# The low halves of the experts' weights, all made on VectorE instead of half of them on GpSimd

## The chip, the core and the metric

The kernel runs on one core of one Trainium2 chip. The metric is the device time of one execution in microseconds (us).

## What is computed

Sliding-window attention (8 heads, the second four dilated by 4) over 4 sequences of 576 tokens gives `x`, 2304 tokens of 512. Each token goes to the one of 8 experts with the largest logit; the result goes through one more pair of dense layers. Cut to what matters:

```python
for e in range(E):                       # 8 experts, w1[e] 512 x 1024, w2[e] 1024 x 512
    mask = e_idx == e
    h = np.maximum(x[mask] @ w1[e], 0.0)
    out[mask] = gate_w[mask, None] * eom[mask, e, None] * (h @ w2[e])
...
h = x @ w_in                             # second mixture: 512 x 2048, then 2048 x 512
return np.square(np.maximum(h, 0.0)) @ w_out
```

## The kernel before, in words

The program has three stages on the core: attention and routing (to about 140 us of the span), the experts (about 140 to 391 us), and the second mixture (from about 391 us). This document is about the second.

**Two halves of each operand.** TensorE gets every float32 operand as two float16 parts, `hi` (the operand, scaled and rounded) and `lo` (what rounding left over), and makes three products: hi by hi, hi by lo, lo by hi. So the weights of each expert are loaded as float32 and split on the chip while TensorE works on the experts before. That is the background work.

**The experts' order.** The experts are taken by rising number of tokens: rank 0 to rank 7, with 248, 264, 284, 304, 320, 340, 380 and 440 token columns. For each rank (L1115 to L1149) there are two layers:

- layer 1 has 8 steps `f`: 12 matmuls on TensorE (L1121), then `hs` hi on ScalarE (L1124, ReLU) and `hs` lo on VectorE (L1125), then some background work (L1127), and in ranks 1 to 4 one step of the sorted tables (`sorted_tables`, called at L1129: small VectorE operations at L777, L781, L202 to L206, L955 to L998, two on ScalarE, and the 18 products of L993);
- layer 2 has 4 steps `c`: first one block of the next rank's tokens is transposed on TensorE (L938) and split (L940 on ScalarE, L941 on VectorE), then 24 matmuls (L1142), which run through all eight `f` of `hs`, three for each, in rising order, then the output's hi on ScalarE (L1147) and lo on VectorE (L1148), then background work (L1149). 

The gathers of the next rank's tokens (L930) are issued from GpSimd's queue at the start of layer 1.

**The background work.** A *unit* is one layer of one rank (u0, u1 for rank 0, u2, u3 for rank 1, and so on), cut into four *pieces* of 128 x 1024 float32, here written u3.1 for piece 1 of unit 3. A piece is loaded by a DMA of SyncE's queue (L307) into one of four stage buffers, which are used in turn, so that the load of a piece waits until the piece four before it has been split. `split_ops` (L278) knows several ways:

- "H" (units 0 and 1): two halves, each hi on ScalarE (L294) and lo on VectorE (L295);
- "D": the whole piece at once, `hi = scale * t` on ScalarE (L294), `lo = scale * t - hi` on VectorE (L295, one scalar_tensor_tensor);
- "Q": ScalarE scales the stage buffer in place (L282), ScalarE copies it to hi (L287), GpSimd subtracts, `lo = t - hi` (L288). Those are two entries in the list of background work, where D is one.

`unit` (L1047) chooses at L1052. The weights of the second mixture's first layer (S pieces, `piece64`, four entries each: L324, L328, L332 on VectorE, L337 on ScalarE with L338 on VectorE) are put between them.

**What sets the order.** Each engine runs its instructions in program order. `Stream.to` (L261) puts the background entries into the program: after step `f` or `c` of a layer, that fraction of the entries of the layer's list is issued. So on VectorE the order in a step `f` is: `hs` lo, the background's, the table step. On ScalarE: `hs` hi, the background's.

```python
def on_pool(n):                                   # L284
    nc.scalar.activation(out=half(hi, n), in_=sv, func=AF.Copy)                                   # L287
    nc.gpsimd.tensor_tensor(out=half(lo, n), in0=sv, in1=half(hi, n), op=ALU.subtract)            # L288
def on_dve(n):                                    # L291
    nc.scalar.activation(out=half(hi, n), in_=sv, func=AF.Copy, scale=scale)                      # L294
    nc.vector.scalar_tensor_tensor(out=half(lo, n), in0=sv, scalar=scale, in1=half(hi, n), ...)   # L295
ops = {..., "D": [on_dve(None)], "H": [on_dve(0), on_dve(1)], "Q": [scaled, on_pool(None)]}       # L298
```

Of the kernel before, what the change touches and what calls it, by code (L numbers as in the profile page):

```python
# [12 lines left out]
I32 = mybir.dt.int32  # L13
# [11 lines left out]
HH = H // 2            # heads per mask type  # L25
WIN = 32               # keys per query
DIL = 4
SEG = S // DIL         # dilated heads: tokens ordered by residue, SEG per residue
QB = 64                # queries per score block
KW = QB + WIN          # keys per score block  # L30
NM = S // QB
NT = B * S
NB = NT // P           # token blocks
# [5 lines left out]
# A round of the mixture takes experts by rising number of tokens, this many tokens at most of each;  # L39
# rounds follow until every expert's tokens are done. Where the first caps do, one round does.  # L40
CAPS = ((248, 264, 284, 304, 320, 340, 380, 440), (256, 272, 296, 320, 344, 368, 416, 512))
CAP = CAPS[1]
CM = -(-max(CAP) // P)                                    # blocks of an expert's tokens in a round
NC = E * CM
NR = max(-(-(NT // (E - r)) // CAP[r]) for r in range(E)) # rounds at most
XW = NT + max(CAP)

# Float32 operands go through the tensor engine as two float16 parts, hi + lo,
# of the operand times a power of two that centres it in float16's range.
X_S = 64.0             # x  # L50
WG_S = 64.0            # logits carry X_S * WG_S
W1_S = 32.0            # h then carries X_S * W1_S
W2_S = 64.0
Y_S = X_S * W1_S * W2_S
Y2_D = 1.0 / 64.0      # y into the second MoE
# [8 lines left out]
# The attention's steps as the engines get them, which overlaps blocks of queries, sequences, and the routing of  # L64
# the blocks that are done: step.number, +products that only keep the tensor engine busy, :engine.
# Loads: LQ of a head pair's q or k, LV of a block's values, GT of the gates' weights.
# A head pair's q or k: QI puts its heads side by side, T transposes a half, TC copies it out.
# A block of queries: S scores (SA, SB: by kind of head), MX maxima, EX exponentials, PT, PC their transpose.
# A block of tokens: PV output, XN division by the sums, ST store, XT transpose, XE, XL its two parts (0, 1: by kind).
# Routing: LG, LE logits, CE early blocks' experts, CC their counts, RC their places, F one-hot places, L0-L2 late logits.  # L70
# [40 lines left out]
def fused_kernel(ctx: ExitStack, tc: tile.TileContext, q, k, v, w_gate, w_ogate, w1, w2, w_in, w_out, out):  # L111
# [16 lines left out]
    # routing: logits by token, and what it is worked out with  # L128
    def bc(ap, n):
        """a column for each of n more elements"""  # L130
        return ap.unsqueeze(len(ap.shape)).to_broadcast(list(ap.shape) + [n])

    def rows(ap, n):
        """[P, m] for each of n blocks"""
        return ap.unsqueeze(1).to_broadcast([P, n, ap.shape[1]])

    L = const.tile([P, NB, 2 * E], F32, name="L")
    d = const.tile([P, NB, E], F32, name="d")             # logit - largest
    cand = const.tile([P, NB, E], F32, name="cand")
    mxl = const.tile([P, NB], F32, name="mxl")  # L140
    oh = const.tile([P, NB, E], F16, name="oh")           # 1 at the token's expert
    iota = const.tile([P, 32], F32, name="iota")
    iota_h = const.tile([P, P], F16, name="iota_h")
    iota_n = const.tile([P, E], F32, name="iota_n")       # e - E
    tokc = const.tile([P, NB], F32, name="tokc")          # token - NT/2, exact in float16
    tokp = const.tile([P, 1], F32, name="tokp")           # token in its block
    ones_h = const.tile([P, P], F16, name="ones_h")
    tri_h = const.tile([P, P], F16, name="tri_h")         # [k, m] = 1 where k < m
    A = const.tile([P, NB, P], F16, name="A")             # one-hot place in the block, times the token
    pm = cand  # L150
    rin = const.tile([P, NB], F32, name="rin")            # tokens of the token's expert before it: P * xi + pl
# [3 lines left out]
    s = const.tile([P, NB], F32, name="s")                # the token's place among experts' blocks  # L155
    Bs = const.tile([P, NB, NC], F16, name="Bs")
    capr = const.tile([P, E], F32, name="capr")           # by rank: most tokens
    thr = const.tile([1, E, 1 + NR], F32, name="thr")     # of the first caps, and those of some rounds of the others

    below = const.tile([1, E, E], F32, name="below")      # [r, r'] = 1 where r' < r  # L160
# [23 lines left out]
    def choose(b, lg):  # L184
        """the expert of the tokens of some blocks: the first with the largest logit"""
# [13 lines left out]
    def halves(x, b=slice(0, NB)):  # L199
        """x = P * xi + pl"""  # L200
        V = nc.vector
        V.tensor_copy(out=xi[:, b], in_=x[:, b])  # L202
        yield
        V.tensor_scalar(out=xi[:, b], in0=xi[:, b], scalar1=7, scalar2=None, op0=ALU.arith_shift_right)
        yield
        V.scalar_tensor_tensor(out=pl[:, b], in0=xi[:, b], scalar=float(-P), in1=x[:, b], op0=ALU.mult, op1=ALU.add)  # L206
        yield

    def places(ts=range(NB), eng="DVE"):
        """one-hot places in the block"""  # L210
# [9 lines left out]
    def blocks_in(b=slice(0, NB)):  # L220
        """one-hot blocks, by expert, times the token"""
# [11 lines left out]
    # x in DRAM, rows by token  # L233
# [3 lines left out]
    def dil_runs(c0, n):  # L237
        """pieces of dilated order c0..c0+n within one sequence: (offset, residue, j, length)"""
# [8 lines left out]
    class Stream:  # L247
        """pieces of work, each a load and the operations on it; loads run ahead of the operations"""
# [14 lines left out]
        def to(self, part, frac):  # L263
            """a part's work up to this fraction of it; the parts before it are done"""
# [7 lines left out]
    def split_ops(st, hi, lo, view, scale, path):  # L272
        """hi, lo: the two parts' places; view: of the staged piece"""
# [27 lines left out]
    def piece(src, hi, lo, view, scale, path="H", stage=None):  # L301
        """1024 float32 columns to load and split"""
# [7 lines left out]
    def piece64(src, hi, lo, scale):  # L310
        """512 float64 columns, which come as their bits: to float32 (cut after 24 bits; magnitudes in
        float32's normal range, or 0), and split"""
# [8 lines left out]
        def op0():  # L321
            # sign and top exponent bit stay, 7 exponent bits and the fraction move up
# [20 lines left out]
    def shared_in(wi):  # L343
        """the second mixture's first weights, into wi [P, 2, KC, F2]"""
# [8 lines left out]
    def shared_out(wo):  # L353
        """and its second ones, into wo [P, 2, F2 / P, DM]"""
# [12 lines left out]
    T_EARLY = 3 * S // P                                  # blocks that end before the last sequence  # L367
    early, late = slice(0, T_EARLY), slice(T_EARLY, NB)
    cnts = {}                                             # for each token and expert: tokens of the expert before it

    def count(out, t0, ts):
        """of some blocks' tokens into the counts of the blocks from t0 on that come later"""
# [10 lines left out]
    def rank_in(b):  # L383
        """the token's place among its expert's"""
# [7 lines left out]
    def far_in(b):  # L392
        """tokens behind the first round's blocks"""
# [3 lines left out]
    def mix(*gens):  # L397
        """operations that wait for each other, with others between"""
        gens = list(gens)
        while gens:  # L400
            gens = [g for g in gens if next(g, gens) is not gens]
# [4 lines left out]
    with ExitStack() as actx:  # L406
# [6 lines left out]
        def warm(ps, n):  # L413
            """into a bank whose data comes later: keeps the tensor engine at its full clock where it would wait"""
# [16 lines left out]
        # dilated heads: a block that begins a sequence, one with all its keys in the queries'  # L431
        # residue, or the query (from the block's first) from which on a new residue begins
# [5 lines left out]
        # for the four head pairs of a block: two of banded heads, two of dilated ones  # L438
# [5 lines left out]
        for kind in dict.fromkeys(["start", "band"] + dil_kind):  # L444
            mt = mk_p.tile([P, H // 2, KW], BF16, name=f"mask_{kind}")
            masks[kind] = mt
            if isinstance(kind, int):
                # dilated queries from `kind` on begin a new residue: keys before it are out
                nc.gpsimd.tensor_copy(out=mt, in_=masks["band"])
                for half in halves_of(mt[:, H // 4:, 0:WIN + kind]):  # L450
                    # keep where p < kind
# [5 lines left out]
            for half in halves_of(mt):  # L457
                # query p of the half, key kk: rel = p + off - kk in [0, WIN)
# [13 lines left out]
        def load_qk(b, hp, nm):  # L472
            """heads 2hp, 2hp+1 of sequence b: some consecutive tokens to a partition"""
# [15 lines left out]
        def emit_QI(b, hp, nm, eng):  # L489
            """a token's two heads side by side"""  # L490
# [9 lines left out]
        def t_dst(b, hp, nm, half):  # L500
            """places of the half's tokens in the transposed heads"""
            t = qkt[b, nm][:, hp, :]
            if hp < 2:
                # token 6p + 3 half + i
                return t.rearrange("p (a r) -> p r a", r=6)[:, 3 * half:3 * half + 3, :]
            # token 8p + 4 half + i: residue i, place 2p + half
# [26 lines left out]
        def emit_S(b, m, w=0, part=None):  # L533
            """scores; of the first blocks, the banded heads' first"""
# [48 lines left out]
        def emit_PV(t, types=range(2)):  # L583
            """two blocks side by side"""
# [22 lines left out]
        def pair_pieces(t):  # L607
            """the two halves of a block: (row offset, rows, sequence, first place in it)"""
# [32 lines left out]
        def xT_parts(ps, o, n, b, c0, types):  # L641
            """places of a piece of a block, with the tokens in order"""
# [16 lines left out]
        # for the logits: pieces of a block within one sequence, but for the late blocks  # L659
# [21 lines left out]
        def late_logits(b, parts):  # L681
            """of the late blocks of a sequence, by parts; all of them are one group"""
# [71 lines left out]
    tok_p = ctx.enter_context(tc.tile_pool(name="tok", bufs=1))  # L754
    perm_i = tok_p.tile([P, NB], U32, name="perm_i")      # token at each sorted place
    gs = tok_p.tile([P, NB], F32, name="gs")              # output scale of each sorted place
# [502 lines left out]
```

## Time and profile before

| | |
|---|---|
| time of the kernel before, median of 3 runs | 772.98 us (771.99 to 773.34) |
| span of the profiled execution, first to last instruction (its own time is not given apart from it) | 771.4 us |
| mean granted TensorE clock over the span | 0.973 of full speed |
| experts' stage, ranks 1 to 7 | 176.7 to 391.7 us |

A row of the timeline gives the start in us from the span's start, the duration in us, the engine (PE is TensorE, DVE is VectorE, ACT is ScalarE, POOL is GpSimd, SPq is SyncE's queue), the line, the operation, and "out<-in" with the shapes; "x24" means that 24 like instructions are merged into the row. In square brackets at the end stands how long the engine had been idle and whose end released it. The profiler's record of a DVE or ACT instruction overlaps the next by about 0.1 us, so the distance from start to start is a little shorter than the duration.

### The profile page before, as it was taken

How to read it: one execution, taken by the hardware profiler on the slowest of the kernel's cores; microseconds unless marked ns; L12 is line 12 of the kernel's file. 1: busy time of each engine (PE TensorE's matmuls, PEld its weight loads, DVE VectorE, ACT ScalarE, POOL GpSimd, SP SyncE). 2: the span in 40 equal slices, each digit the busy share in tenths (PEclk: the TensorE clock that was granted, in tenths of full speed). 3: DMA queues.
4: the chain of work that ended last, by engine and by line, in shares of the span. 5: the costliest groups of instructions: out<-in, count | busy, mean ns of one | idle time of the engine just before them, and what ended most of it. 6: DMA issues, size and time to landing. Idle time of an engine off the chain costs nothing.

```text
span 771.4 us, 13668 instructions
## 1 busy us (share of the span) xinstructions
PE 732.8 (95%) x5380; PEld 446.2 (58%) x5380; DVE 361.4 (47%) x745; ACT 402.1 (52%) x799; POOL 131.4 (17%) x145
## 2 busy tenths in 40 slices
PE   7989998598978999999999999999999999999996
PEld 6877887377756676665544444444444444476442
DVE  3667678478777677577656776002200221011000
ACT  5876777276755777664257777017700672054000
POOL 8000002206435364351000000100000000000000
PEclk7999999599999999999999999999999999999999
DMA  9986543656556576675243330000000000000000
GB/s 211 201 217 148 140 105 99 218 191 212 181 190 192 181 247 196 198 238 165 65 131 97 112 92 1 27 28 1 0 14 28 14 1 14 27 16 1 27 28 27
DMA packets 74968, 82.57 MB, mean 107 GB/s; under 512 B 33784, under 2 KB 57848, under 8 KB 74896
## 3 DMA queue, kind: packets, MB, share of 16 engines
q1 hardware_dynamic: 71552, 71.61, 32.0%
q0 software_dynamic: 3344, 10.01, 3.7%
q8 instruction: 44, 0.72, 0.4%
q14 instruction: 28, 0.23, 0.1%
HBM read 72.16 MB, written 9.44 MB: 106 GB/s over the span
## 4 chain that ended last, share of the span: by engine, by line
PE 82%; DVE 7%; DMA 5%; ACT 3%; issue 2%; SPq 0%; POOLq 0%; DVEq 0%; ACTq 0%
PE bank L1195 24%; PE bank L1212 23%; PE bank L1142 12%; PE bank L1121 9%; PE sps L545 3%; PE tps L571 3%; PE tps L517 2%; PE xps L590 2%; DVE wu L295 2%; DMA vt<-in_v_dram 2%; PE bank L938 1%; DVE hs L1125 1%; PE tps L630 1%; DMA xg<-x_dram,slot_i 1%; DVE rt L777 1%
## 5 line engine op out<-in xcount | busy, mean ns | idle before, releaser
L1195 PE MATMUL bank<-x,wi 128*128 128x512 f16 (+1 forms) x960 | 187.4, 358 | 0.7 <-DVE dec L332 0.7
L1212 PE MATMUL bank<-wo,gg 128*128 128x512 f16 x864 | 187.1, 379 | 0.0
L1195 PEld LDWEIGHTS <-wi 128*128 128x128 f16 x960 | 93.8, 98 | 93.9 <-PE bank L1142 1.1
L1212 PEld LDWEIGHTS <-gg 128*128 128x128 f16 x864 | 84.6, 98 | 101.7
L1142 PE MATMUL bank<-hs,wu 128*128 128x248 f16 (+7 forms) x768 | 113.0, 304 | 9.1 <-DVE hs L1125 8.6
L1121 PE MATMUL bank<-xs,wu 128*128 128x248 f16 (+7 forms) x768 | 109.5, 305 | 1.5 <-ACT wu L294 0.7
L1203 DVE TENSOR_TENSOR gg<-A,gg 128x512 f16<-128x512 f32 (+1 forms) x40 | 25.5, 638 | 169.2 <-ACT gg L1202 169.0
L1142 PEld LDWEIGHTS <-wu 128*128 128x128 f16 x768 | 75.6, 99 | 41.1 <-issue 10.2
L1121 PEld LDWEIGHTS <-wu 128*128 128x128 f16 x768 | 76.2, 100 | 33.2 <-ACT wu L294 1.0
L288 POOL TENSOR_TENSOR wu<-stage,wu 128x1024 f16<-128x1024 f32 x28 | 60.0, 2146 | 120.9 <-ACT wu L287 81.6
L295 DVE SCALAR_TENSOR_TENSOR wu<-stage,wu 128x1024 f16<-128x1024 f32 (+1 forms) x40 | 54.3, 1365 | 21.4 <-ACT wu L294 20.1
L1217 POOL DMA_INDIRECT out_dram<-A,perm_i x9 | 8.7, 969 | 308.5 <-ACT A L1216 308.5
L1216 ACT ACTIVATE wk<-bank,gs 128x512 f32<-128x512 f32 x9 | 6.2, 687 | 87.1 <-PE bank L1212 87.1
L1216 ACT ACTIVATE A<-bank,gs 128x512 f32<-128x512 f32 x9 | 6.2, 687 | 78.9 <-PE bank L1212 78.9
L1203 DVE TENSOR_TENSOR gg<-wk,gg 128x512 f16<-128x512 f32 (+1 forms) x40 | 25.5, 638 | 46.2 <-ACT gg L1202 46.0
L562 ACT ACTIVATE pr<-sps,mx 128x96 f32<-128x96 f32 x144 | 37.0, 345 | 12.0 <-DVE mx L553 8.6
L1124 ACT ACTIVATE hs<-bank 128x248 f16<-128x248 f32 (+7 forms) x64 | 27.6, 434 | 27.3 <-PE bank L1121 27.3
L294 ACT ACTIVATE wu<-stage 128x1024 f16<-128x1024 f32 (+1 forms) x40 | 36.6, 923 | 5.5 <-DMA stage<-in_moe_w_dram 5.5
L1125 DVE SCALAR_TENSOR_TENSOR hs<-bank,hs 128x248 f16<-128x248 f32 (+7 forms) x64 | 30.4, 485 | 14.2 <-ACT hs L1124 14.1
L545 PE MATMUL sps<-kT,qT 64*64 64x96 f32 x576 | 33.2, 256 | 0.0
L1147 ACT ACTIVATE x<-bank 128x248 f32 (+7 forms) x32 | 14.1, 440 | 34.6 <-PE bank L1142 34.4
L282 ACT ACTIVATE stage<-stage 128x1024 f32<-128x1024 f32 x28 | 29.4, 1051 | 4.2 <-DMA stage<-in_moe_w_dram 3.7
(178 smaller groups left out, 852.3 us busy)
## 6 DMA issues: line engine op xcount, KB each, us to landing
stage<-in_moe_w_dram SPq DMA_DIRECT2D x62, 512.0 KB
dstage<-in_moe_w_in_dram SPq DMA_DIRECT2D x16, 512.0 KB
dstage<-in_moe_w_out_dram SPq DMA_DIRECT2D x16, 512.0 KB
vt<-in_v_dram SPq DMA_DIRECT2D x56, 96.0 KB
q<-in_q_dram SPq DMA_DIRECT2D x16, 288.0 KB
k<-in_k_dram SPq DMA_DIRECT2D x16, 288.0 KB
x_dram<-xn SPq DMA_DIRECT2D x22, 128.0 KB
hs<-in_moe_w_dram SPq DMA_DIRECT2D x2, 512.0 KB
```

The costliest lines, as they stand in the source:

```text
L282: nc.scalar.activation(out=t, in_=t, func=AF.Copy, scale=scale)
L288: nc.gpsimd.tensor_tensor(out=half(lo, n), in0=sv, in1=half(hi, n), op=ALU.subtract)
L294: nc.scalar.activation(out=half(hi, n), in_=sv, func=AF.Copy, scale=scale)
L295: nc.vector.scalar_tensor_tensor(out=half(lo, n), in0=sv, scalar=scale, in1=half(hi, n), op0=ALU.mult, op1=ALU.subtract)
L545: nc.tensor.matmul(out=ps[rows, hp, :], lhsT=qt[rows, hp, q0:q0 + QB], rhs=kt[rows, hp, k0:k0 + KW], start=False, stop=hp == H // 2 - 1)
L562: nc.scalar.activation(out=pr[:, hp, :], in_=ps[:, hp, :], func=AF.Exp, bias=mx[:, hp:hp + 1])
L1121: nc.tensor.matmul(out=ps, lhsT=w[:, a, k, f * P:(f + 1) * P], rhs=x[:, k, 0:C], start=nn == 0, stop=nn == 3 * KC - 1)
L1125: V.scalar_tensor_tensor(out=hs[:, 1, f, 0:C], in0=ps, scalar=0.0, in1=hs[:, 0, f, 0:C], op0=ALU.max, op1=ALU.subtract)
L1142: nc.tensor.matmul(out=ps, lhsT=w[:, a, f, c * P:(c + 1) * P], rhs=hs[:, o, f, 0:C], start=nn == 0, stop=nn == 3 * (F // P) - 1)
L1195: nc.tensor.matmul(out=ps, lhsT=wi[:, a, kc, f * P:(f + 1) * P], rhs=x2[o][:, kc, toks], start=nn == 0, stop=nn == 11)
L1203: nc.vector.tensor_tensor(out=lo, in0=r, in1=hi, op=ALU.subtract)
L1212: nc.tensor.matmul(out=ps, lhsT=gg[gi % 2][:, f, a, (j - g0) * P:(j - g0 + 1) * P], rhs=wo[:, o, f, :], start=nn == 0, stop=nn == 3 * (F2 ...
```

## The change

Pieces 1 and 3 of every unit from u2 on are split in the way D instead of the way Q. All 28 instructions of L288 on GpSimd and all 28 of L282 on ScalarE go; L287 becomes L294; 28 more instructions of L295 stand in VectorE's queue. A unit's list of background entries has 4 instead of 6, so `Stream.to` spreads them anew. The lines keep their numbers (comments are blanked).

```diff
     def unit(u, e_regs, stages=()):
         """weights of a rank's layer: its pieces"""
         r, layer = divmod(u, 2)
         res = []
         for i in range(4):
-            path = "DQ"[i % 2] if u >= 2 else "H"
+            path = "D" if u >= 2 else "H"
             st = stages[i] if i < len(stages) else None
```

The entries issued behind each step, ranks 1 and 2 (a piece in brackets is on GpSimd, in two entries; S0 is the first S piece; "-" is a step without one):

```
rank 1 layer 1, f 0..7  before  [u3.1 | u3.1] | u3.2 | [u3.3 | u3.3] | u4.0 | [u4.1 | u4.1]
                        after   - | u3.1 | - | u3.2 | u3.3 | - | u4.0 | u4.1
rank 1 layer 2, c 0..3  before  u4.2 S0 | S0 S0 S0 | [u4.3 u4.3] | u5.0 [u5.1 u5.1]
                        after   u4.2 S0 | S0 S0 | S0 u4.3 | u5.0 u5.1
rank 2 layer 1, f 0..7  before  - | u5.2 | [u5.3 | u5.3] | u6.0 | [u6.1 | u6.1] | u6.2
                        after   - | u5.2 | - | u5.3 | u6.0 | - | u6.1 | u6.2
```

## Rows read from the trace of the kernel before

**Rows 1.** The page, part 1: busy us, share of the span, instructions.

```profile
PE 732.8 (95%) x5380; PEld 446.2 (58%) x5380; DVE 361.4 (47%) x745; ACT 402.1 (52%) x799; POOL 131.4 (17%) x145
```

**Rows 2.** Waits of PE from 130 to 420 us: total us, times, longest.

```profile
PE bank L1142 <- DVE hs L1125: 8.6, 8, 2.5
```

**Rows 3.** Timeline of PE, ranks 1 to 3.

```profile
187.48 0.60 PE L938 MATMUL bank<-identf,xg 128*128 128x128 f32 x4
...
198.97 5.57 PE L1142 MATMUL bank<-hs,wu 128*128 128x264 f16 x48
204.38 11.76 PE L1121 MATMUL bank<-xs,wu 128*128 128x284 f16 x96
215.98 0.60 PE L938 MATMUL bank<-identf,xg 128*128 128x128 f32 x4
...
224.00 0.63 PE L1142 MATMUL bank<-hs,wu 128*128 128x284 f16 x2 [2.47 <-DVE hs L1125]
...
229.65 5.97 PE L1142 MATMUL bank<-hs,wu 128*128 128x284 f16 x48
235.46 4.81 PE L1121 MATMUL bank<-xs,wu 128*128 128x304 f16 x36
242.33 0.92 PE L993 MATMUL bank<-rt,A 128*128 128x90 bf16 x18 [2.05 <-DVE rt L777]
...
255.78 0.42 PE L1142 MATMUL bank<-hs,wu 128*128 128x304 f16 x2 [1.50 <-DVE hs L1125]
```

**Rows 4.** Windows of PE: stretch, its length, PE busy, PEclk, DMA share, GB/s.

```profile
224.00:228.00 4.00, 4.00 (x21) 0.59 0.70 243
240.00:244.00 4.00, 1.95 (x29) 1.00 0.79 237
```

**Rows 5.** L288 and L295: count, ns min/median/max, first and last start.

```profile
L288 POOL TENSOR_TENSOR wu<-stage,wu x28: 2126/2134/2434, 172.8 to 354.6; 128x1024 f16<-128x1024 f32 x28
...
L295 DVE SCALAR_TENSOR_TENSOR wu<-stage,wu x40: 675/1220/3746, 157.1 to 352.5; 128x1024 f16<-128x1024 f32 x28, 128x512 f16<-128x512 f32 x12
```

**Rows 6.** Timeline of POOL, rank 1.

```profile
183.93 1.43 POOL L930 DMA_INDIRECT xg<-x_dram,slot_i  x1 [0.30 <-PE bank L1121]
185.39 4.22 POOL L288 TENSOR_TENSOR wu<-stage,wu 128x1024 f16<-128x1024 f32 x2
```

**Rows 7.** Timeline of DVE, ranks 1 to 3.

```profile
179.18 2.32 DVE L295 SCALAR_TENSOR_TENSOR wu<-stage,wu 128x1024 f16<-128x1024 f32 x1 [1.47 <-ACT wu L294]
...
181.76 0.21 DVE L777 TENSOR_TENSOR rt<-rt,rt 128x64 f32<-128x64 f32 x1
...
183.04 0.42 DVE L1125 SCALAR_TENSOR_TENSOR hs<-bank,hs 128x264 f16<-128x264 f32 x1
183.38 1.22 DVE L295 SCALAR_TENSOR_TENSOR wu<-stage,wu 128x1024 f16<-128x1024 f32 x1
...
185.14 4.51 DVE L204 TENSOR_SCALAR xi<-xi 128x18 int32<-128x18 int32 x1
...
192.68 0.73 DVE L955 TENSOR_SCALAR A<-iota_h,pl 128x128 bf16<-128x128 f16 x4
...
208.65 2.10 DVE L955 TENSOR_SCALAR A<-iota_h,pl 128x128 bf16<-128x128 f16 x4
...
213.80 3.00 DVE L777 TENSOR_TENSOR rt<-rt,iota 128x324 bf16<-128x324 bf16 x1
...
223.42 0.18 DVE L986 CAST rt<-rt 128x18 bf16<-128x18 f32 x1
...
238.00 2.37 DVE L295 SCALAR_TENSOR_TENSOR wu<-stage,wu 128x1024 f16<-128x1024 f32 x1 [1.44 <-ACT wu L294]
...
253.28 2.06 DVE L295 SCALAR_TENSOR_TENSOR wu<-stage,wu 128x1024 f16<-128x1024 f32 x1 [0.47 <-ACT wu L294]
```

**Rows 8.** Timeline of ACT, rank 1.

```profile
191.63 1.06 ACT L282 ACTIVATE stage<-stage 128x1024 f32<-128x1024 f32 x1 [2.42 <-DMA stage<-in_moe_w_dram]
```

**Rows 9.** Timeline of SyncE's queue, rank 1.

```profile
187.56 0.99 SPq L307 DMA_DIRECT2D stage<-in_moe_w_dram  x2
```

## The prediction

> **What bounds the kernel now.** I read the busy shares first: TensorE is busy 95% of the span, VectorE 47%, GpSimd 17% [rows 1]. Those are averages over stages; what the change is worth is read where TensorE waits in the experts' stage. Its waits there come next: the largest is L1142, layer 2, for the low part of `hs` from VectorE (L1125), 8.6 us in 8 waits [rows 2]. The timeline of TensorE puts them into ranks 1, 2 and 3 alone: from rank 4 on it has no gap until the last rank's end. So VectorE, idle half the time on the whole, is late in three ranks, where the steps of the sorted tables stand in its queue too.
>
> What the gaps cost is more than the waits. Rank 1: from the first transpose of layer 2 at 187.48 to layer 1 of rank 2 at 204.38 are 16.9 us [rows 3]. Its last 48 matmuls take 204.38 - 198.97 = 5.41, so 96 take 10.8, and three groups of transposes (0.60 by the record, about 0.4 from start to start) 1.2: 12.0 unhindered, so 4.9 are lost. Rank 2 in the same way: 215.98 to 235.46 is 19.5; 48 matmuls take 5.81; 2 x 5.81 + 1.2 = 12.8; 6.7 are lost. [...] After the wait at 224.00 the way to 229.65 is 5.65 us, where 26 matmuls at 0.121 and two groups of transposes would take 3.95: the clock cost 1.7 of the 6.7. Rank 3 loses its two waits, 2.05 and 1.50 [rows 3]. **In all 4.9 + 6.7 + 3.55 = 15.1 us are there to be won.**
>
> **Why VectorE is late.** An L295 of 128x1024 takes 1.22 us by the median but up to 3.75 [rows 5], and small table operations take 3.00 and 4.51 [rows 7]. Set beside GpSimd's timeline each of these ends with an L288, or one of its own lengths behind it: GpSimd's two subtractions run from 185.39 to 189.61 [rows 6], and L204, 18 columns, stands from 185.14 to 189.65. In ranks 1 to 3 I count 11 such rows, the first at 179.18, the last at 253.28 [rows 7]; less what the same operation takes alone (1.22 for L295, 0.2 for L204) they lose 18.7 us: 5.4 in rank 1 ahead of the last `hs` lo (1.1 at 179.18, 4.3 at 185.14), 5.9 in rank 2 up to its last one.
>
> **The change, part by part.**
>
> *GpSimd:* 28 subtractions of 2.13 us go [rows 5]. Nothing is slower for it: its queue keeps the gathers, which now start without a subtraction ahead of them.
>
> *VectorE, added:* 28 L295 at 1.22, 34.2 us; start to start 1.14, since a record overlaps the next by 0.08 (`hs` lo of 0.42 at 183.04, the next at 183.38 [rows 7]). In ranks 1 to 3 these are 14, 16.0 us, against 18.7 of stalls that go. From rank 4 on some 1.2 us in each step with a former Q piece lie in VectorE's idle time; without that cover they would cost TensorE at most the same.
>
> *ScalarE:* two instructions become one, 28 x 1.06 us less [rows 8]. This lets the first D of a rank start about 0.95 earlier.
>
> *Loads:* a stage buffer was free only when GpSimd had done its piece, behind the gathers [rows 6]. So the load of u4.1 was issued at 187.56 [rows 9] and ScalarE, with the last `hs` hi behind it, waited for it until 191.63 [rows 8], 4.1 later. Now u3.1 is done at about 182.0; the load lands near 186, ahead of ScalarE's turn at 188.0.
>
> *Rank 1, replayed:* its first D (u3.0) started at 179.18 behind two ScalarE instructions, one of which goes: 178.2, 1.5 us after layer 1 begins. Up to the last `hs` lo VectorE then has 5 D (u3.0 to u3.3, u4.0), 5.7; 8 `hs` at 0.34, 2.7; the table steps from 181.76 to 192.68, 10 rows, 2.9 without stalls; about 0.5 waiting for ScalarE between. That ends at 190.0. TensorE wants it at its 23rd matmul of layer 2, 187.9 + 22 x 0.113 = 190.4. No wait, with 0.4 to spare: 4.9 to 0.
>
> *Rank 2:* layer 1 begins 4.9 earlier, at T = 199.5. VectorE starts u5.0 at T + 1.5; then 6 D (u5.0 to u6.1), 6.8; 8 `hs` at 0.37, 3.0; table steps from 208.65 to 223.42, 18 rows, 4.8 without stalls. The last `hs` lo is ready at T + 16.1. TensorE wants it at T + 11.6 (215.98 - 204.38) + 0.4 + 22 x 0.121 = T + 14.7. A wait of 1.4 stays; gaps of 1.5 and 2.05 in rank 3 left the clock whole [rows 4], so I charge nothing for it: 6.7 to 1.4. **This is what is late next.**
>
> *Rank 3:* L993 waited 2.05 for a table step behind the L295 of 238.00. That loses 1.14 of stall and 0.95 on ScalarE and gets one more D, 1.14, ahead of it: 1.1 stays. The second wait, 1.50, loses 0.83 of stall (253.28) and two ScalarE instructions, about 2, for one more D: none.
>
> **Sum.** 15.1 - (0 + 1.4 + 1.1) = 12.6 us less. The profiled span of 771.4 becomes 758.8. Only the span of that execution is given; the median of the runs, 772.98, lies 1.6 above it, which I take as what lies around it, unchanged: **760.4 us**. The bounds of the unknown: at best all 15.1 go (757.9); the unproved price is how full VectorE's queue is in ranks 1 and 2, where the replay has 0.4 to spare. A measurement of this kernel tells some 0.2%, 1.5 us, from no change.
>
> **Rivals.**
>
> A. *The queue is tighter than replayed.* If loads land late or the stalls' work returns as waits between VectorE and ScalarE, and the last `hs` lo comes 2 us later in both ranks: rank 1 loses 1.6, rank 2 another 2.0 and the clock's 1.7. Gain 12.6 - 5.3 = 7.3: **765.7**. For it: margins of a few tenths out of 12 us. Against it: records overlap, so that my sums err upward.
>
> B. *Part of the stalls is not the subtractions' doing.* In the row of L204 VectorE began at 185.14, 0.25 before GpSimd's pair, and a gather (to 185.36) was running [rows 6, 7]. The same holds for L777 at 213.80. If what blocks stays, the 4.3 in rank 1 leaves 3.9 (0.4 to spare), the 2.5 in rank 2 stays, and the clock's 1.7: 12.6 - 8.1 = 4.5, **768.5**. Against it: the gather ends at 185.36 and can explain 0.2 of 4.3; L204 ends 0.04 after the second subtraction. [...]
>
> C. *VectorE becomes the bound: slower.* The place is its queue ahead of the last `hs` lo in ranks 1 to 3. If the long rows are no port stall at all, the added D come on top: 2 in rank 1 (2.3), 3 in rank 2 (3.4), in rank 3 one ahead of L993 and one more ahead of the last `hs` (2.3): 8.0 us, **781.0**. It decides where less stall goes than work comes: under 2.3 of 5.4 in rank 1, under 3.4 of 5.9 in rank 2, with nothing from ScalarE. For it: these are the ranks where VectorE is late already. Against it: 11 rows that end with a subtraction. [...]
>
> D. *No change to be measured*, a balance of C's work and B's rest. That the change does not do what it says can be left out: odd pieces from u2 on are all that reaches L288.
>
> **How the numbers follow.** The forecast gets 0.58, A 0.20, B 0.08, D 0.05, C 0.09. Faster by over 0.2%: 0.58 + 0.20 + 0.08 = 0.86; within: 0.05; slower: 0.09. The range begins at 757.0 (all 15.1 won, and 0.9 for the spread of the runs) and reaches over A and B with the same spread to 769.5; C and D are left out, 0.14, and a little more for errors of size.
>
> **What would show it.** Right: L295 never above 1.3 us; L204 near 0.2; GpSimd with gathers alone; TensorE's waits for `hs` lo down from 8.6 to about 1.4, in rank 2 only, and that for L993 to about 1.1; the clock at 1.00 from 176 to 225 us; ScalarE's busy time some 29 us lower, VectorE's only a few us higher (34 added, most of it given back). Wrong: long L295 or table rows without GpSimd beside them (B, C); `hs` lo late in rank 1 with VectorE never idle since 178 (A, C); ScalarE waiting for loads in rank 1 as at 191.63 (A); a gap in rank 4 or later, which would mean that VectorE's idle time there was no cover.

## The result, and the profile after

The changed kernel takes 759.19 us (median; 758.63 to 760.03) against 772.98: a ratio of 0.9829, 95% interval 0.9800 to 0.9859. That is 13.8 us faster; 12.6 were forecast, 760.4 us.

The page of the changed kernel, part 1, and TensorE's waits in the experts' stage, in the columns of [rows 1] and [rows 2]:

```profile
PE 728.1 (96%) x5380; PEld 443.1 (58%) x5380; DVE 363.7 (48%) x773; ACT 375.5 (50%) x771; POOL 67.3 (9%) x117
...
PE bank L1142 <- DVE hs L1125: 1.5, 1, 1.5
...
PE bank L993 <- DVE rt L777: 1.2, 1, 1.2
```

TensorE's eight waits of 8.6 us for `hs` lo are one of 1.5. VectorE, which got 34 us of work, is busy only 2.3 us longer than before: what it used to lose waiting beside GpSimd was counted as busy. So busy time in these profiles can be waiting: L204 counted 4.51 us [rows 7] where it takes 0.17 here.

The timeline of TensorE, ranks 1 to 3, to be set beside [rows 3]:

```profile
175.81 10.96 PE L1121 MATMUL bank<-xs,wu 128*128 128x264 f16 x96
186.61 0.60 PE L938 MATMUL bank<-identf,xg 128*128 128x128 f32 x4
...
193.33 5.57 PE L1142 MATMUL bank<-hs,wu 128*128 128x264 f16 x48
198.74 11.76 PE L1121 MATMUL bank<-xs,wu 128*128 128x284 f16 x96
210.34 0.60 PE L938 MATMUL bank<-identf,xg 128*128 128x128 f32 x4
...
215.06 0.40 PE L1142 MATMUL bank<-hs,wu 128*128 128x284 f16 x2 [1.45 <-DVE hs L1125]
...
224.91 4.81 PE L1121 MATMUL bank<-xs,wu 128*128 128x304 f16 x36
230.94 0.92 PE L993 MATMUL bank<-rt,A 128*128 128x90 bf16 x18 [1.21 <-DVE rt L777]
231.70 7.91 PE L1121 MATMUL bank<-xs,wu 128*128 128x304 f16 x60
239.45 0.60 PE L938 MATMUL bank<-identf,xg 128*128 128x128 f32 x4
```

Layer 2 of rank 1 now takes 198.74 - 186.61 = 12.1 (16.9 before), that of rank 2 224.91 - 210.34 = 14.6 (19.5 before). Rank 1 has no gap; the two that are left are those that the prediction named. From the start of rank 1 to the first matmul of the second mixture it is 378.56 - 175.81 = 202.75 us, and 215.0 before (176.68 to 391.70). This stretch, called the **stage** below, is what I compare between profiles: its beginning lies between 174.6 and 178.2 us in the profiles of this study, and little that was edited stands ahead of it (of the 28 subtractions one, at 172.76). It holds 12.3 of the 13.1 us by which the spans differ. A second profile of the changed kernel (run 8) has it at 202.2, so differences of about half a microsecond tell nothing.

L295 by its source view, and the timeline of VectorE:

```profile
L295 DVE SCALAR_TENSOR_TENSOR wu<-stage,wu x68: 679/1224/1226, 156.0 to 340.6; 128x1024 f16<-128x1024 f32 x56, 128x512 f16<-128x512 f32 x12
```

```profile
177.36 1.23 DVE L295 SCALAR_TENSOR_TENSOR wu<-stage,wu 128x1024 f16<-128x1024 f32 x1 [0.53 <-ACT wu L294]
...
183.92 0.17 DVE L204 TENSOR_SCALAR xi<-xi 128x18 int32<-128x18 int32 x1
...
188.68 0.42 DVE L1125 SCALAR_TENSOR_TENSOR hs<-bank,hs 128x264 f16<-128x264 f32 x1
...
206.80 0.48 DVE L777 TENSOR_TENSOR rt<-rt,iota 128x324 bf16<-128x324 bf16 x1
...
214.56 0.45 DVE L1125 SCALAR_TENSOR_TENSOR hs<-bank,hs 128x284 f16<-128x284 f32 x1
```

The longest L295 is 1.226 us where it was 3.75 [rows 5]; L204 takes 0.17 where it took 4.51, and that L777 0.48 instead of 3.00 [rows 7]. The granted clock stays at 1.00 through rank 2's gap of 1.45, in the columns of [rows 4]:

```profile
212.00:216.00 4.00, 2.55 (x23) 1.00 0.76 247
216.00:220.00 4.00, 4.00 (x36) 1.00 0.83 261
```

The load of u4.1 is issued at 181.33, where it was 187.56 [rows 9], and ScalarE takes it up at 187.09 without waiting for it.

### The profile page after: what moved, and what is told of

The parts are those of the page before. It is cut to its first block, busy times and chain, and to the rows that moved or that the text cites. A ratio compares the mean times of both kernels' runs of the same rounds, so it can differ in the third digit from the quotient of the medians.

```text
span 758.3 us, 13692 instructions
## 1 busy us (share of the span) xinstructions
PE 728.1 (96%) x5380; PEld 443.1 (58%) x5380; DVE 363.7 (48%) x773; ACT 375.5 (50%) x771; POOL 67.3 (9%) x117
## 4 chain that ended last, share of the span: by engine, by line
PE 85%; DMA 8%; DVE 3%; issue 2%; ACT 1%; POOLq 0%; ACTq 0%; SPq 0%
PE bank L1195 25%; PE bank L1212 23%; PE bank L1142 13%; PE bank L1121 12%; DMA q<-in_q_dram 3%; DMA vt<-in_v_dram 3%; PE sps L545 3%; PE xps L590 2%; PE tps L571 2%; PE bank L938 1%; DVE wu L295 1%; PE tps L517 1%; PE tps L630 1%; DMA xg<-x_dram,slot_i 1%; DMA k<-in_k_dram 1%
## 5 line engine op out<-in xcount | busy, mean ns | idle before, releaser
L1142 PE MATMUL bank<-hs,wu 128*128 128x248 f16 (+7 forms) x768 | 109.6, 300 | 2.1 <-DVE hs L1125 1.5
L1142 PEld LDWEIGHTS <-wu 128*128 128x128 f16 x768 | 74.5, 98 | 32.0 <-issue 1.6
L295 DVE SCALAR_TENSOR_TENSOR wu<-stage,wu 128x1024 f16<-128x1024 f32 (+1 forms) x68 | 75.8, 1128 | 12.0 <-ACT wu L294 10.7
L294 ACT ACTIVATE wu<-stage 128x1024 f16<-128x1024 f32 (+1 forms) x68 | 65.3, 975 | 2.0 <-DMA stage<-in_moe_w_dram 2.0
L562 ACT ACTIVATE pr<-sps,mx 128x96 f32<-128x96 f32 x144 | 37.0, 346 | 13.3 <-DVE mx L553 10.0
L1125 DVE SCALAR_TENSOR_TENSOR hs<-bank,hs 128x248 f16<-128x248 f32 (+7 forms) x64 | 31.2, 489 | 15.9 <-ACT hs L1124 15.8
L930 POOL DMA_INDIRECT xg<-x_dram,slot_i x24 | 25.5, 1061 | 145.1 <-PE bank L1142 103.2
L545 PEld LDWEIGHTS sps<-kT,qT 64*64 64x64 f32 x576 | 25.9, 137 | 8.6 <-issue 8.2
```

The lines of the kernel that those rows point to most:

```text
L545: nc.tensor.matmul(out=ps[rows, hp, :], lhsT=qt[rows, hp, q0:q0 + QB], rhs=kt[rows, hp, k0:k0 + KW], start=False, stop=hp == H // 2 - 1)
L562: nc.scalar.activation(out=pr[:, hp, :], in_=ps[:, hp, :], func=AF.Exp, bias=mx[:, hp:hp + 1])
L930: nc.gpsimd.indirect_dma_start(out=xg[n % 4][0:w], out_offset=None, in_=x_dram, in_offset=bass.IndirectOffsetOnAxis(ap=slot_i[0:w, CM * r ...
L1125: V.scalar_tensor_tensor(out=hs[:, 1, f, 0:C], in0=ps, scalar=0.0, in1=hs[:, 0, f, 0:C], op0=ALU.max, op1=ALU.subtract)
L1142: nc.tensor.matmul(out=ps, lhsT=w[:, a, f, c * P:(c + 1) * P], rhs=hs[:, o, f, 0:C], start=nn == 0, stop=nn == 3 * (F // P) - 1)
```

## Experiments

The theory: VectorE's stalls beside GpSimd's subtraction make `hs` lo late. The rivals: ScalarE's second instruction makes `hs` hi late; the stage buffers come free late; the entries are spread better. The first five runs take these parts; run 1 takes the stalls and the late buffers together. Times are medians; ratios are to the kernel before on the same chip (771.29, 771.63 and 772.23 us in the three groups of runs).

**1. Only the engine of the subtraction.**

```diff
-                nc.gpsimd.tensor_tensor(out=half(lo, n), in0=sv, in1=half(hi, n), op=ALU.subtract)
+                nc.vector.tensor_tensor(out=half(lo, n), in0=sv, in1=half(hi, n), op=ALU.subtract)
```

> Edit to the kernel before: only the subtraction of the Q pieces moves from GpSimd to VectorE; ScalarE still scales in place and copies, and the background entries are spread as before. Theory (VectorE's stalls beside GpSimd's subtraction are the main cause of the gaps): the gaps of ranks 1 and 2 go nearly as in the changed kernel, ScalarE's extra instruction puts back about 0.95 us into rank 2 and at L993 each, so about 761 us, at most 763. Rival (the second ScalarE instruction, which delays hs hi, is the main cause): most of the gaps stay, 768 us or more. Rival (the new spreading of the entries is the cause): 768 us or more as well.

Measured: 762.7 us, ratio 0.9899 (0.9868 to 0.9931). The subtraction on VectorE takes 1.22 us, as L295 does. TensorE's waits:

```profile
PE bank L993 <- DVE rt L777: 2.3, 1, 2.3
PE bank L1142 <- DVE hs L1125: 2.2, 2, 1.9
```

Rank 1 has no gap, rank 2's is 2.2. The stage is 206.7 us. So 8.3 of the 12.3 us come with the subtraction's engine alone, ScalarE doing what it always did. They hold a second effect, though: GpSimd no longer keeps the stage buffers, and ScalarE, which waited 6.8 us for loads in ranks 1 to 7 before, does not wait for one here.

**2. The stalls put back.** Edit to the changed kernel, shortened; the constant is spread to the shape of `hi`:

```diff
+        def with_junk():
+            on_dve(None)()
+            nc.gpsimd.tensor_tensor(out=junk, in0=constant, in1=hi, op=ALU.subtract)
...
-            path = "D" if u >= 2 else "H"
+            path = "DG"[i % 2] if u >= 2 else "H"       # G: with_junk
```

> Edit to the changed kernel: behind the hi of each former Q piece GpSimd does a subtraction of 1024 columns that nobody waits for (a constant minus the piece's hi, into a scratch tile; its result is not used). ScalarE, loads and spreading stay as in the changed kernel. Theory: rows of VectorE with one or two SBUF inputs are long again and end with GpSimd's; about 5 us of stall ahead of the last hs lo in rank 1 and 5 in rank 2 come back as gaps, with the clock's loss some 12 to 18 us: 771 to 777 us, since VectorE now has the added pieces and the stalls. Rival (ScalarE or the loads are the cause): 759 to 761 us.

Measured: 781.79 us, ratio 1.015 (1.0109 to 1.0192), 22.6 over the changed kernel's 759.19, which is from another group of runs. The stage is 224.2 us, 21.5 longer. TensorE's waits (lines are a few higher in this kernel: L1151 is L1142, L1134 is L1125, L297 is L295), VectorE and GpSimd in rank 1:

```profile
PE bank L1151 <- DVE hs L1134: 16.1, 13, 2.8
```

```profile
182.89 3.81 DVE L297 SCALAR_TENSOR_TENSOR wu<-stage,wu 128x1024 f16<-128x1024 f32 x1
186.63 2.10 DVE L204 TENSOR_SCALAR xi<-xi 128x18 int32<-128x18 int32 x1
188.65 0.42 DVE L1134 SCALAR_TENSOR_TENSOR hs<-bank,hs 128x264 f16<-128x264 f32 x1
```

```profile
175.05 3.11 POOL L304 TENSOR_TENSOR junk<-identf,wu 128x1024 f16<-128x1024 f32 x1 [3.62 <-ACT wu L296]
...
183.47 7.43 POOL L304 TENSOR_TENSOR junk<-identf,wu 128x1024 f16<-128x1024 f32 x3
```

And at 231.62, where no gather runs near (the one before began at 215.26, the next at 242.67):

```profile
231.62 3.07 DVE L297 SCALAR_TENSOR_TENSOR wu<-stage,wu 128x1024 f16<-128x1024 f32 x1
```

```profile
231.48 2.12 POOL L304 TENSOR_TENSOR junk<-identf,wu 128x1024 f16<-128x1024 f32 x1 [5.61 <-ACT wu L296]
```

A subtraction that nobody waits for makes VectorE's rows long again and costs some 22 us. That shows the cause: in the experts' stage of this trace no wait of TensorE, VectorE, ScalarE or SyncE's queue ends with a GpSimd instruction, so nothing joins the two engines but that they run side by side. It cost more than the 12 to 18 expected; VectorE now has the added pieces as well as the stalls, and gaps of 1.9 and 2.6 appear in ranks 4 and 5, which had none before the change.

**3. The same, holding the stage buffer.** The unused subtraction reads the piece's stage buffer instead of a constant (`in0=st["t"]`).

> As the run with the unused GpSimd subtraction, but it reads the stage buffer of the piece, as the removed one did, so that the buffer is free only when GpSimd is done, behind its gathers. Theory: the loads add little to the stalls, 0 to 3 us over the run without the hold. Rival (late loads are the larger part): 5 us or more over it.

Measured: 783.49 us (1.0169, 1.0115 to 1.0223), 1.7 over the run before it, the intervals overlapping; the stages are 224.6 and 224.2 us. The hold does what it should: ScalarE waits 7.5 us for loads, and never in the run before it. Beside the stalls, buffers that come free late are thus not a large part. What they cost without the stalls this run can't show; run 6 does, for rank 1.

**4. ScalarE's relief alone.** Edit to the kernel before:

```diff
-        ops = {..., "Q": [scaled, on_pool(None)]}
+        ops = {..., "Q": [hi_only, lo_on_pool]}      # ScalarE: hi = t; GpSimd: lo = t - hi
```

The kernel leaves out the scaling of these pieces, so both of their halves lack the scale.

> Edit to the kernel before: ScalarE's scaling in place of the Q pieces is left out (their lo and hi lack the scale, so part of the output is off by it), one ScalarE instruction instead of two; GpSimd still subtracts, the entries are spread as before. Theory: VectorE's stalls beside GpSimd stay, so ScalarE's relief alone brings 0 to 4 us: 767 to 772 us. Rival (ScalarE's second instruction is the larger part of the gain): 764 us or less.

Measured: 769.85 us, ratio 0.9973 (0.9952 to 0.9993); the stage is 212.2 us, 2.8 less. TensorE still waits 5.9 us for `hs` lo (5 times) and 2.7 at L993. A small part, as the theory has it.

**5. The old spreading.** Edit to the changed kernel:

```diff
+        ops = {..., "E": [lambda: None, on_dve(None)]}
...
-            path = "D" if u >= 2 else "H"
+            path = "DE"[i % 2] if u >= 2 else "H"
```

> Edit to the changed kernel: each former Q piece has two background entries again, the first of them empty, so the pieces are spread as before the change. Theory: the spreading matters little, 758 to 761 us. Rival (the new spreading brought the gain): 765 us or more.

Measured: 761.02 us, ratio 0.9876 (0.9842 to 0.9909): at the edge of what was expected. The stage is 205.7 us, 2.9 longer than in the changed kernel, and the profile says where. Rank 3 on TensorE, and the clock there:

```profile
232.75 1.36 PE L993 MATMUL bank<-rt,A 128*128 128x90 bf16 x18 [2.29 <-DVE rt L777]
233.89 9.16 PE L1121 MATMUL bank<-xs,wu 128*128 128x304 f16 x60
```

```profile
232.00:236.00 4.00, 3.25 (x27) 0.63 0.74 238
```

The old spreading puts three L295 ahead of the table step instead of two, 1.1 us more of wait at L993; after 2.29 us the clock was granted at 0.63, and the 60 matmuls behind it took 9.16 where they took 7.91. Together 2.3 of the 2.9.

Runs 1 and 5 and the changed kernel make a chain from before: 215.0, 206.7 (subtraction on VectorE), 205.7 (and ScalarE once), 202.75 us (and the new spreading). So 8.3, 1.0 and 2.9 us, in this order, from one profile each; the 1.0 is little more than two profiles of one kernel differ by. The medians of run 5 and of the changed kernel are 1.8 apart, in different groups, and their intervals overlap. But run 1, which has the old spreading too, shows the same at L993: a wait of 2.26, and the clock at 0.83 and 0.75 in the two windows from 232 to 240 us.

**6. Table steps later, in both kernels.** `if 1 <= r < 5` becomes `if 3 <= r < 7`. The changed kernel:

> Edit to the changed kernel: the steps of the sorted tables stand in ranks 3 to 6 instead of 1 to 4. Theory: the two gaps that stayed (1.45 before the last hs lo of rank 2, 1.21 before L993) came from VectorE's queue with the table steps in it; in later ranks a step f is longer and VectorE has idle time. The first goes, the second goes or moves with L993 to rank 5: 756 to 758 us. Rival (the queue of added pieces alone makes the gap of rank 2): 759 us.

Measured: 759.24 us, ratio 0.9841 (0.9805 to 0.9878): no gain, and outside the 756 to 758 expected. It is the rival's time, but not its mechanism: rank 2's gap is gone, so the added pieces alone did not make it. But

```profile
283.19 0.92 PE L993 MATMUL bank<-rt,A 128*128 128x90 bf16 x18 [1.86 <-DVE rt L777]
```

the wait at L993 came along to rank 5 and grew from 1.21 to 1.86. The stage is 202.1, too near to 202.75 and 202.2 to tell. The kernel before:

> Edit to the kernel before: the steps of the sorted tables stand in ranks 3 to 6. Theory (stalls, in a queue made full by the table steps; beside it the load of u4.1 that is late behind GpSimd): about half of the gain, since the long table rows fall where VectorE has idle time, while the late load of rank 1 stays: 762 to 768 us. Rival (stalls cost as much wherever they stand): 770 us or more. Rival (the table steps alone were the cause): 760 us or less.

Measured: 777.3 us, ratio 1.0071 (1.0043 to 1.0098): slower, and the expectation wrong; the rival that stalls cost as much elsewhere holds. TensorE waits 8.0 us for VectorE's `hs` lo and 2.8 for ScalarE's hi, the longest wait for a lo being 4.4 us in rank 3. VectorE and ScalarE there:

```profile
235.08 2.91 DVE L332 SCALAR_TENSOR_TENSOR dec<-dstage,dec 128x512 uint32<-128x512 uint32 x1
```

```profile
238.02 0.63 ACT L337 ACTIVATE wi<-dec 128x512 f16<-128x512 f32 x1 [4.62 <-DVE dec L332]
238.56 0.41 ACT L1124 ACTIVATE hs<-bank 128x304 f16<-128x304 f32 x1
```

In the later ranks the S pieces stand in the queues too. A stalled L332 (2.91 for 0.69) holds up ScalarE's L337, and `hs` hi behind it in program order: the stall reaches TensorE by two engines.

But only 0.8 of the 2.8 us for ScalarE's hi are in rank 3. The other 2.0 are in rank 1, and come from the late load, which this kernel still has. ScalarE and TensorE there:

```profile
189.51 1.06 ACT L282 ACTIVATE stage<-stage 128x1024 f32<-128x1024 f32 x1 [2.43 <-DMA stage<-in_moe_w_dram]
190.48 0.37 ACT L1124 ACTIVATE hs<-bank 128x264 f16<-128x264 f32 x1
```

```profile
190.90 0.27 PE L1142 MATMUL bank<-hs,wu 128*128 128x264 f16 x1 [2.01 <-ACT hs L1124]
```

With the table steps out of rank 1, TensorE waits 0.6 us there for VectorE and 2.0 because of the load, which had been expected to stay late.

**7. GpSimd that only writes.** Edit to the changed kernel: `nc.gpsimd.memset(st["t"], 0.0)` behind each former Q piece.

> Edit to the changed kernel: behind each former Q piece GpSimd fills the piece's stage buffer with zeros once VectorE has read it (the load that follows writes over it). GpSimd then only writes to SBUF. If what blocks VectorE is GpSimd's reading, L295 (two operands from SBUF) stays at 1.2 us beside it and the time is 759 to 763 us (the buffers are held a little longer); if any access of GpSimd blocks it, L295 rows of up to the fill's length come back.

Measured, in a single run: 763.83 us. GpSimd and VectorE in ranks 2 and 4 (L958 is L955):

```profile
203.37 0.95 POOL L300 MEMSET stage<- 128x1024 f32 x1 [2.43 <-DVE wu L295]
...
271.63 0.95 POOL L300 MEMSET stage<- 128x1024 f32 x1 [3.21 <-issue]
```

```profile
203.59 1.00 DVE L958 TENSOR_SCALAR A<-iota_h,pl 128x128 bf16<-128x128 f16 x4
...
271.92 1.23 DVE L295 SCALAR_TENSOR_TENSOR wu<-stage,wu 128x1024 f16<-128x1024 f32 x1
```

The fill from 271.63 to 272.58 does not lengthen the L295 that begins at 271.92, with two operands from SBUF; no L295 of this run is over 1.23 us, with 28 fills, where beside subtractions they took up to 3.75 [rows 5]. The one-operand L958 from float16 to bfloat16 is longer beside a fill: four take 1.00 here, 0.98 at 186.29 and 1.26 at 191.09, and 0.74 at 188.97, where no fill runs. So the subtraction lengthens L295 and the fill does not. That it is the subtraction's reading is my estimate: the two differ in length as well, 2.13 and 0.95 us. The time is 0.8 above the 759 to 763 expected for that case, in one execution.

**8. Taking the last two gaps.** Edit to the changed kernel: `yield` twice ahead of the products of L993, so that they are issued two steps later; in one run alone, in another with the tables in ranks 3 to 6. The changed kernel ran beside them.

> Edit to the changed kernel: the table steps in ranks 3 to 6, and the 18 products of L993 two steps later than the VectorE step that they need. Theory: TensorE meets L993 in program order, so a wait there is the distance from VectorE's step to the products; two steps more take it to 0. With rank 2's gap gone too, 2.0 to 2.7 us under the changed kernel of the same call. Rival (what goes there comes back at another step): within 1 us of it.

> Edit to the changed kernel: only the products of L993 two steps later, the tables where they were. Theory: the wait of 1.21 at L993 goes, rank 2's of 1.45 stays: about 1.2 us under the changed kernel.

> The changed kernel as it is, for a comparison on the same chip: 758 to 761 us.

Measured: 756.84 us (ratio 0.9790, 0.9764 to 0.9815) with both, 757.88 (0.9802, 0.9776 to 0.9829) with the later products alone, 759.09 (0.9815, 0.9785 to 0.9845) for the changed kernel. The medians lie 2.25 and 1.2 apart as expected, while the intervals overlap. The profiles are clearer. With both, TensorE has no gap at the products, and none for `hs` in any rank:

```profile
279.31 8.81 PE L1123 MATMUL bank<-xs,wu 128*128 128x340 f16 x60
287.96 0.91 PE L995 MATMUL bank<-rt,A 128*128 128x90 bf16 x18
288.71 5.35 PE L1123 MATMUL bank<-xs,wu 128*128 128x340 f16 x36
```

The stages are 200.1, 200.9 and 202.2 us. The changed kernel's two waits recur at 1.45 and 1.21 us in this second profile of it. The version with both edits has the lowest median of the study.

## Why the prediction was right

- **Where the gaps were, and why.** Right, and shown from both sides: run 2 puts the stalls back and nothing that another engine waits for; run 1 takes them away, together with the late loads, and leaves ScalarE and the spreading as they were.
- **Rank 1, 4.9 to 0.** Measured 16.9 - 12.1 = 4.8. The replay had the last `hs` lo end 13.3 us after the rank begins (190.0 - 176.7); it ends at 189.10 - 175.81 = 13.3.
- **Rank 2, 6.7 to 1.4.** The wait is 1.45 and the clock stays at 1.00, as forecast; [rows 4] show that for the gap of 2.05 alone, and from 256 to 260 us, behind that of 1.50, it was 1.00 too. What the clock cost is gone: the 24 matmuls behind the gap take 3.06 us, and 4.06 before, in the window granted 0.59 [rows 4]. The layer is 4.9 shorter where 5.3 were forecast. The replay's T + 16.1 measured 215.01 - 198.74 = 16.3.
- **Rank 3.** The wait at L993 is 1.21 for a forecast 1.1; the second is gone. From rank 4 on TensorE has no gap, as forecast, though VectorE's added pieces go on there.
- **The sum.** The stage is 12.3 shorter for a forecast 12.6. The other 0.8 us of the span lie ahead of it: it begins 0.87 earlier. Its beginning differs by more than that between the profiles of this study, so none of it can be given to the change.
- **The busy times.** ScalarE has 26.6 us less (some 29 forecast), VectorE 2.3 more ("a few").
- **A term that was not priced by itself:** the new spreading of the entries. The replay used it, so the sum had it, but the prediction put the whole gain down to stalls, ScalarE and loads. Run 5's profile puts 2.9 of the 12.3 on it, through the wait at L993 and the clock behind it.
- **The loads.** Right that they bind rank 1, and not priced by themselves. In the kernel before the stalls hid them: the last `hs` hi of rank 1 was done at 192.96, and its lo, behind a table step, began at 193.33. Run 6 takes the table steps out of rank 1, and there the late load costs TensorE the 2.01 us shown. So 4.9 to 0 in rank 1 needed both, the stalls gone and the load early. How the 8.3 us of run 1 divide between the two stays open: no run takes the stalls away and leaves the buffers held.
- **Rival C** (slower, VectorE the bound) has nearly the time of run 2, 781.0 for 781.8, but that is chance: its condition was that the long rows are no stall beside GpSimd, and in run 2 they are just that, with the added pieces on top. The prediction calls the long rows a port stall; no run shows a port, only rows of VectorE that are long beside GpSimd's subtractions. And 28 subtractions of 2.13 us on GpSimd cost TensorE more than 28 of 1.22 on VectorE: it waits 8.6 us for `hs` lo before, 2.2 in run 1.
- **Rival B** (the stalls not the subtractions' doing) falls with run 2, where the L297 at 231.62 is long beside a subtraction with no gather near; L204 at 0.17 agrees, though no gather runs beside it in the changed kernel.
- **Rivals A and D** fall: the last `hs` lo came within 0.2 us of the replay in both ranks, and the gain is far above the 1.5 us that a measurement can tell.

## What to carry to other kernels

Before work is put on a second engine "for nothing", look at the longest instance of the first engine's instructions beside their median, and at what ends them: here 3.75 us for 1.22, the long ones ending with the other engine's, or one of their own lengths behind it. A stall costs what it delays in the critical engine's program order, so replay the queue up to the one instruction that the critical engine waits for, instead of adding up busy times. And products that need a small result are best issued a few steps after it: two steps took the 1.21 us out of run 8's profile, and no new wait came.

## What had not been expected of the hardware

- In run 2 either engine is lengthened beside the other. L304 takes 3.11 us instead of 2.13 where an L297 had begun 0.11 before it, at 174.94, and ended at 176.17. Yet L297 at 182.89 began 0.58 before GpSimd's three at 183.47, while a gather ran, and took 3.81 for 1.22; and L204 before, begun 0.25 ahead of GpSimd's pair, took 4.51 for 0.17 [rows 6, 7]. By the recorded starts, then, the one that begins first keeps its time in the first case and not in the other two. Whether the gather ahead of it matters stays open.
- Beside a GpSimd instruction that only writes, the two-operand L295 keeps its time, 1.23 us at most for a median of 1.22, and four of the one-operand L958 take 0.98 to 1.26 instead of 0.74 (run 7).
- The gathers, without subtractions ahead of them in GpSimd's queue, run far earlier: in the changed kernel the three for rank 2 begin at 149.49, 164.00 and 168.20 us, where they began at 180.57, 182.68 and 183.93. TensorE waits for no gather in ranks 1 to 7 of either kernel.
- The granted clock fell after some single gaps: to 0.83 and 0.75 in the windows at and behind one of 2.26 us (run 1), to 0.63 at one of 2.29 (run 5), to 0.92 and 0.66 at and behind one of 2.38 (run 6). Behind one of 2.29 in run 7, 24 matmuls took 4.73 us where the changed kernel's take 3.06. It stayed at 1.00 after 1.21 (the changed kernel). Behind 2.11 (run 7, rank 3), 2.36 (run 6, rank 4), 2.64 (run 2, rank 5) and 2.66 us (run 4, rank 3) the matmuls kept the times that they have in the changed kernel: 60 in 7.91, 24 in 3.42, 24 in 3.62 and 60 in 7.91 us. So the length of the gap alone does not tell; what does stays open.
